# Loading two interleaved streams from two DMA queues instead of one

## The chip, the cores and the metric

The kernel runs on one core of a Trainium2 chip. The metric is the time of one execution on the device in microseconds (us). Most executions of one kernel agree within about 0.3%, so a few us of 2036 can only be judged from several runs, and stage times are read from one profiled run each. Before and the later run e4, whose traces show the same order of instructions and loads up to the end of pass 2, differed by 1.2 us at the end of pass 1 and by 2.8 us at the end of pass 2; a difference of stage times under some 3 us is not counted as shown.

Engine names are those of the profile: PE is the matmul engine (PEld its weight loads), DVE and ACT do elementwise work, POOL is GpSimd, SP is SyncE. DMA requests are made by an engine's instruction stream. A request waits there, in order, until its destination buffer is free. "Landing" is the moment when the load's last part has been reported.

## The reference

The kernel computes the output and all gradients of two rounds of attention and a squared-ReLU MLP, for one token. Nearly all bytes are the two caches, 67 MB each.

```python
def _A_ref(x, k_cache, v_cache, wq, wo):           # 32 query heads, 4 KV heads, 65536 keys, head size 128
    q = (x @ wq).reshape(B, Sq, Hq, Dh).transpose(0, 2, 1, 3)
    scores = jnp.einsum("bhqd,bhkd->bhqk", q, repeat(k_cache)) * (Dh ** -0.5)
    o = jnp.einsum("bhqk,bhkd->bhqd", _softmax(scores), repeat(v_cache))
    return o.transpose(0, 2, 1, 3).reshape(B, Sq, Hq * Dh) @ wo

def _fwd_reference(...):
    x = x + _A_ref(_layernorm(x), A_k_cache, A_v_cache, A_wq, A_wo)
    x = x + _B_ref(_layernorm(x), B_w1, B_b1, B_w2, B_b2)      # 1024 -> 3584 -> 1024
    x = x + _A_ref(_layernorm(x), A_k_cache, A_v_cache, A_wq, A_wo)
    x = x + _B_ref(_layernorm(x), B_w1, B_b1, B_w2, B_b2)
# result: x, and the vjp of this function for grad_out (gradients of both caches are 67 MB each, too)
```

## The kernel before

It makes four passes over the caches: two forward ones, a backward one that only loads (pass 3), and a backward one that loads and stores both cache gradients (pass 4). Between the passes there are dense stages for the MLP. Every big load is 1 MB and goes into one of 12 slots of the same size; 7 blocks are kept from one pass to the next. All loads are requested by SyncE.

```python
    def kv8(t, g, c8):                              # eight chunks of the K or V block that holds chunk c8
        b, j = divmod(c8, J)                        # J = 32 chunks of 128 rows in a block of 1 MB
        key = (t, g, b)
        if key not in KV["have"]:
            sl = Slot("blk_" + t)
            v = sl.t[:, :].rearrange("p (j d) -> p j d", d=DH)
            nc.sync.dma_start(out=v, in_=KVIN[t][g][b])
            KV["have"][key] = (sl, v)
        return KV["have"][key][1][:, j:j + 8, :]

    def slabs(name, load, nk, kper, ncols, ahead=1):            # wq, wo, w1, w2 in 1 MB slabs
        ...
            sl = Slot(name)
            v = sl.t[:, 0:kn * ncols].rearrange("p (k n) -> p k n", n=ncols)
            nc.sync.dma_start(out=v, in_=load(k, kn))
        ...
```

In the forward passes each step transposes eight chunks of K (kT), multiplies the ones before by the queries (kS), and multiplies much older ones by V (v8). FWD_LAG is 23 steps, so the V block of a chunk is needed 23 steps of eight chunks after its K block. A background generator (bg) slips in the matmuls of the projections with wq and wo of the other head groups, whose slabs come by the same queue.

```python
        def kT(g, c8):
            ...
            kb8 = kv8("k", g, c8)
            for i in range(8):
                nc.tensor.transpose(pt[:, i, :], kb8[:, i, :], ident_b[:, :])      # L774
            ...
        def v8(g, c8):
            vb8 = kv8("v", g, c8)
            ...
                nc.tensor.matmul(ps_o[:, 0:w, :], lhsT=vb8[:, i, :], ...)            # L858
        ...
        KV["keep"] = plan_keep(p)
        pipeline(items, [(kT, 0), (kS, TLEAD), (v8, FWD_LAG)], bg, end)
```

Pass 3 does the same with V first and K later. Each engine works through its stream in order; a scheduler of the language decides the order of the instructions on each engine at build time, from its own idea of when data arrive.

## Time and profile before

| | before |
|---|---|
| time, median of 3 | 2037.67 us (2037.56 to 2038.18) |
| passes 1, 2 and 3 (profiled run): first transpose to last product | 12.5 to 378.1, 433.3 to 781.2, 833.3 to 1197.7 us |
| DMA rate in these passes, whole slices | 406 to 416 GB/s |
| PE busy | 83% of the span |

The first view is the page of the kernel before: the mean busy share of the DMA engines and what they moved in 40 slices of 51 us each; then the two queues (q1 takes SyncE's requests, q0 GpSimd's) with packets, MB and share; then the issues with their number, KB and the median us from issue to landing.

```profile
...
DMA  9999999999999998999999986999999999999995
GB/s 384 416 410 414 413 414 415 360 335 406 411 414 413 413 415 323 398 415 410 416 412 414 416 338 231 375 424 393 422 424 424 423 423 404 423 415 423 423 371 212
...
q1 hardware_dynamic: 112190, 633.39, 76.9%
q0 software_dynamic: 24048, 165.70, 19.6%
...
blk_k<-in_A_k_cache_dram SPq DMA_DIRECT2D x248, 1024.0 KB, 20.1
blk_v<-in_A_v_cache_dram SPq DMA_DIRECT2D x243, 1024.0 KB, 20.2
...
s_wq<-in_A_wq_dram SPq DMA_DIRECT2D x32, 1024.0 KB, 18.8
s_wo<-in_A_wo_dram SPq DMA_DIRECT2D x32, 1024.0 KB, 20.2
...
```

The reader is to see two things. In passes 1 to 3 (slices 1 to 6, 9 to 14 and 17 to 22, counted from 0) the DMA is full and moves 406 to 416 GB/s. And these loads land some 20 us after their request: one queue serves loads in the order in which they were requested, with eight in flight at 2.5 us each.

The next view is what SyncE's stream waited for between 20 and 375 us of the kernel before, that is in pass 1 (us in total, times, longest).

```profile
...
SPq L282 <- DMA blk_k<-in_A_k_cache_dram: 92.4, 48, 3.2
SPq L282 <- DMA blk_v<-in_A_v_cache_dram: 73.6, 43, 2.3
SPq L282 <- PE ps_tr L774: 47.8, 36, 5.4
...
```

SyncE waits mostly for its own earlier loads, because eight are in flight, and for PE to free slots. The third view is what PE waited for between 20 and 800 us, passes 1 and 2 and the dense stages at them; only the waits for a DMA are shown.

```profile
...
PE ps_mv L397 <- DMA s_w<-in_B_w_dram: 9.0, 6, 2.4
...
PE ps_acc L858 <- DMA blk_v<-in_A_v_cache_dram: 3.8, 5, 1.5
...
PE ps_tr L774 <- DMA blk_k<-in_A_k_cache_dram: 3.3, 3, 1.4
...
```

The last view is PE's timeline at the end of pass 1 (start, us, engine, line, what, and in brackets the idle time ahead of it with its releaser).

```profile
...
358.56 0.61 PE L774 MATMUL ps_tr<-ident_b,blk_k 128*128 128x128 bf16 x8
...
374.90 1.89 PE L858 MATMUL ps_acc<-E,blk_v 128*128 128x64 bf16 x32
377.05 1.06 PE L858 MATMUL ps_acc<-E,blk_v 128*128 128x64 bf16 x32 [0.26 <-DMA blk_v<-in_A_v_cache_dram]
...
```

The last V block landed at 377.0 us, PE stood ready for it, and the pass was over 1.1 us later. The end of pass 2:

```profile
...
776.96 1.89 PE L858 MATMUL ps_acc<-E,blk_v 128*128 128x64 bf16 x32 [1.50 <-DMA blk_v<-in_A_v_cache_dram]
779.45 1.72 PE L858 MATMUL ps_acc<-E,blk_v 128*128 128x64 bf16 x32 [0.60 <-DMA blk_v<-in_A_v_cache_dram]
...
```

### The profile page before, as it was taken

Reading aid. Unit: us, or ns where it says so; the run is one execution under the profiler, and the core shown is the slowest. Engines: PE = TensorE matmul, PEld = TensorE weight load, DVE = VectorE, ACT = ScalarE, POOL = GpSimd, SP = SyncE. Lnnn points to the kernel's source line nnn. Section 1 sums busy time; section 2 is a strip of 40 time slices with the busy share of each in tenths; the row PEclk is TensorE's granted clock in tenths of the full one; section 3 lists DMA queues with packets and bytes.
Section 4 is the critical chain, followed back from the end, with each engine's and each line's share of the span. In section 5 each row is a group of like instructions: output and inputs, shape, how many; then the busy total and the mean of one; then the engine's idle time right before and its main releaser. Section 6 shows DMA issues by size and latency. Waiting matters only on the chain.

```text
span 2035.9 us, 69009 instructions
## 1 busy us (share of the span) xinstructions
PE 1689.3 (83%) x30754; PEld 1344.3 (66%) x30754; DVE 1188.6 (58%) x2586; ACT 1103.0 (54%) x2063; POOL 92.4 (5%) x232
## 2 busy tenths in 40 slices
PE   7888887688788886887978888979988978898897
PEld 6778777688787776776867777545544545454454
DVE  4444454255444542555464446867967877687775
ACT  3544454255444542445354345767766766576675
POOL 0000000000000000000000000101101111010111
PEclk9999899799899996999999988988988998698898
DMA  9999999999999998999999986999999999999995
GB/s 384 416 410 414 413 414 415 360 335 406 411 414 413 413 415 323 398 415 410 416 412 414 416 338 231 375 424 393 422 424 424 423 423 404 423 415 423 423 371 212
DMA packets 136536, 803.50 MB, mean 395 GB/s; under 512 B 12448, under 2 KB 12462, under 8 KB 52398
## 3 DMA queue, kind: packets, MB, share of 16 engines
q1 hardware_dynamic: 112190, 633.39, 76.9%
q0 software_dynamic: 24048, 165.70, 19.6%
q8 instruction: 240, 3.93, 0.8%
q14 instruction: 58, 0.48, 0.1%
HBM read 633.35 MB, written 165.69 MB: 392 GB/s over the span
## 4 chain that ended last, share of the span: by engine, by line
PE 45%; DMA 28%; ACT 15%; DVE 8%; issue 4%; SPq 0%; ACTq 0%; POOLq 0%; DVEq 0%; POOL 0%
DMA blk_v<-in_A_v_cache_dram 13%; PE ps_tr L774 7%; ACT E L831 6%; DMA blk_k<-in_A_k_cache_dram 5%; PE ps_sc L792 5%; PE ps_tr L1026 4%; PE ps_gg L1074 4%; PE ps_acc L858 4%; ACT kt L150 4%; PE ps_tr L917 3%; DVE kt L153 3%; DMA out_dram<-og 3%; PE ps_gg L1139 2%; DMA out_dram<-gstk 2%; PE ps_mv L397 2%
## 5 line engine op out<-in xcount | busy, mean ns | idle before, releaser
L153 DVE COPY kt<-ps_tr 128x1024 bf16<-128x1024 bf16 x751 | 507.3, 687 | 340.6 <-PE ps_tr L774 145.4
L150 ACT COPY kt<-ps_tr 128x1024 bf16<-128x1024 bf16 x273 | 275.7, 1024 | 410.9 <-PE ps_tr L774 230.0
L774 PE MATMUL ps_tr<-ident_b,blk_k 128*128 128x128 bf16 x4096 | 297.3, 226 | 4.3 <-DMA blk_k<-in_A_k_cache_dram 3.3
L150 ACT CAST gstk<-ps_gg 128x512 bf16<-128x512 f32 x396 | 207.6, 600 | 99.7 <-PE ps_gg L1074 78.5
L150 ACT CAST gstv<-ps_gg 128x512 bf16<-128x512 f32 x379 | 199.2, 601 | 100.1 <-PE ps_gg L1074 99.2
L774 PEld LDWEIGHTS <-blk_k 128*128 128x128 bf16 x4096 | 249.5, 102 | 4.9 <-DMA blk_k<-in_A_k_cache_dram 3.8
L792 PE MATMUL ps_sc<-L_qpad,kt 128*128 128x64 bf16 (+7 forms) x4096 | 197.4, 194 | 52.8 <-DVE kt L153 38.8
L1074 PE MATMUL ps_gg<-GG,xt 64*128 64x512 bf16 x1024 | 211.5, 403 | 21.2 <-ACT gstk L150 11.0
L792 PEld LDWEIGHTS <-kt 128*128 128x128 bf16 x4096 | 158.8, 100 | 71.3 <-DVE kt L153 45.7
L858 PE MATMUL ps_acc<-E,blk_v 128*128 128x64 bf16 (+4 forms) x4096 | 177.6, 200 | 33.0 <-issue 10.9
L1026 PEld LDWEIGHTS <-blk_v 128*128 128x128 bf16 x2048 | 128.5, 103 | 108.0 <-issue 83.0
L1026 PE MATMUL ps_tr<-ident_b,blk_v 128*128 128x128 bf16 x2048 | 183.0, 230 | 20.1 <-DMA blk_v<-in_A_v_cache_dram 18.9
L858 PEld LDWEIGHTS <-blk_v 128*128 128x128 bf16 x4096 | 152.9, 103 | 36.4 <-issue 31.3
L831 ACT ACTIVATE E<-S_sb,L_negm 128x128 bf16<-128x128 f32 x256 | 150.4, 990 | 38.2 <-DVE L_negm L827 38.1
L1101 PEld LDWEIGHTS <-blk_k 128*128 128x128 bf16 x2048 | 84.3, 100 | 115.7 <-issue 87.0
L917 PE MATMUL ps_tr<-ident_b,blk_v 128*128 128x128 bf16 x2048 | 143.7, 224 | 14.3 <-DMA blk_v<-in_A_v_cache_dram 12.0
L917 PEld LDWEIGHTS <-blk_v 128*128 128x128 bf16 x2048 | 121.4, 100 | 31.1 <-DMA blk_v<-in_A_v_cache_dram 20.6
L1101 PE MATMUL ps_acc<-X,blk_k 128*128 128x64 bf16 (+3 forms) x2048 | 119.2, 196 | 23.0 <-DMA blk_k<-in_A_k_cache_dram 23.0
L831 ACT ACTIVATION_READ_ACCUMULATOR E<-S_sb,L_negm 128x1 f32 x256 | 123.5, 483 | 0.0
L937 PE MATMUL ps_sc<-dOpad,kt 128*128 128x64 bf16 (+7 forms) x2048 | 100.7, 194 | 26.6 <-ACT kt L150 15.5
L1055 PE MATMUL ps_sc<-DOB,kt 128*128 128x64 bf16 (+3 forms) x2048 | 111.3, 198 | 0.2 <-DVE kt L153 0.2
L153 DVE CAST gstv<-ps_gg 128x512 bf16<-128x512 f32 x133 | 90.0, 684 | 28.1 <-PE ps_gg L1074 27.7
(271 smaller groups left out, 2203.0 us busy)
## 6 DMA issues: line engine op xcount, KB each, us to landing
blk_k<-in_A_k_cache_dram SPq DMA_DIRECT2D x248, 1024.0 KB, 20.1
blk_v<-in_A_v_cache_dram SPq DMA_DIRECT2D x243, 1024.0 KB, 20.2
out_dram<-gstv POOLq DMA_DIRECT2D x64, 1024.0 KB, 13.1
out_dram<-gstk POOLq DMA_DIRECT2D x64, 1024.0 KB, 12.5
s_wq<-in_A_wq_dram SPq DMA_DIRECT2D x32, 1024.0 KB, 18.8
s_wo<-in_A_wo_dram SPq DMA_DIRECT2D x32, 1024.0 KB, 20.2
s_w<-in_B_w_dram SPq DMA_DIRECT2D x32, 896.0 KB, 7.8
out_dram<-og POOLq DMA_DIRECT2D x23, 1024.0 KB, 13.9
```

The costliest lines, as they stand in the source:

```text
L150: nc.scalar.copy(out=out, in_=in_)
L153: nc.vector.tensor_copy(out=out, in_=in_)
L774: nc.tensor.transpose(pt[:, i, :], kb8[:, i, :], ident_b[:, :])
L792: nc.tensor.matmul(state["ps_s"][:, s:s + w, :].rearrange("p a b -> p (a b)"), lhsT=kt[:, i, :], rhs=L["qpad"][:, g, 0:w, :].rearrange("p ...
L831: nc.scalar.activation(out=E(g, c0, SU)[:, :, L["lr"].start + h], in_=S[:, h, :], func=ACTF.Exp, bias=negm[:, g, su, h:h + 1], scale=SCALE ...
L858: nc.tensor.matmul(ps_o[:, 0:w, :], lhsT=vb8[:, i, :], rhs=E(g, c, w)[:, :, lr], start=(c % SU == 0), stop=(c % SU == SU - 1), skip_group_ ...
L917: nc.tensor.transpose(pt[:, i, :], vb8[:, i, :], ident_b[:, :])
L937: nc.tensor.matmul(state["ps_dp"][:, s:s + w, :].rearrange("p a b -> p (a b)"), lhsT=vt[:, i, :], rhs=dOpad[:, g, 0:w, :].rearrange("p a b ...
L1026: nc.tensor.transpose(pt[:, i, :], vb8[:, i, :], ident_b[:, :])
L1055: nc.tensor.matmul(state["ps_dp"][:, s:s + w, :].rearrange("p a b -> p (a b)"), lhsT=vt[:, i, :], rhs=DOB[:, g, 0:w, :].rearrange("p a b - ...
L1074: nc.tensor.matmul(pgs[h][:, :], lhsT=xt[64 * h:64 * h + 64, j1 // 8 + m, :], rhs=gg[64 * h:64 * h + 64, :, :].rearrange("p a b -> p (a b) ...
L1101: nc.tensor.matmul(ps_dq[:, 0:w, :].rearrange("p a b -> p (a b)"), lhsT=kb8[:, i, :], rhs=X[:, s:s + w, :].rearrange("p a b -> p (a b)"), ...
```

## The change

The intent: while SyncE's stream waits for a slot or a completion, V loads can go out by a queue of their own. In passes 1 to 3 K blocks and slabs stay on SyncE, V blocks are requested by GpSimd. In pass 4 GpSimd's queue has the stores, so there all loads stay on SyncE.

```diff
-    KV = {"have": {}, "keep": set()}
+    KV = {"have": {}, "keep": set(), "two": True}
 # in kv8
-            nc.sync.dma_start(out=v, in_=KVIN[t][g][b])
+            (nc.gpsimd if t == "v" and KV["two"] else nc.sync).dma_start(out=v, in_=KVIN[t][g][b])
 # in each of the three functions that run a pass
         KV["keep"] = plan_keep(p)
+        KV["two"] = p < 3
```

The build also reorders the other engines' instructions.

More of the change, by code (lines that the diff above doesn't have):

```diff
@@ L967, in attn_bwd3 @@
         KV["keep"] = plan_keep(p)
+        KV["two"] = p < 3
         pipeline(items, [(vT, 0), (vS, TLEAD), (k8, B3_LAG)], bg, end)
@@ L1112, in attn_bwd4 @@
         KV["keep"] = plan_keep(p)
+        KV["two"] = p < 3
         pipeline(items, [(vT, 0), (vS, TLEAD), (dV8, DV_LAG), (k8, B4_LAG)], bg, end)
```

## The prediction

> **What bounds the kernel now.** The windows view gives passes 1 to 3 (about 30-360, 445-765, 840-1180 us) a DMA share of 1.01-1.02 and 408-417 GB/s; pass 4 (1280-2000 us), where GpSimd's queue stores while SyncE's loads, has slices at 423-424. SyncE's issues follow each other every 2.5 us (1 MB at 413 GB/s) and land 20 us later: eight in flight, as many as that queue has completion semaphores, so SyncE waits mostly for its own earlier DMA (215 + 207 us), else for PE to free one of 12 slots (118 + 106 us; waits view). An issue takes 0.33 us on SyncE, 0.53 us on GpSimd. Yet compute is nearly level with the DMA: PE is 80% busy and waits for blocks under 10 us in pass 1, hardly in pass 2, about 30 us in pass 3. Between passes DMA falls to 0.7-0.9 for 70-80 us, because 7 of 12 slots hold kept blocks.
>
> **What changes.** 183 V loads move from SyncE to GpSimd; no byte is saved. The Trainium skill, page "DMA: Bandwidth & Descriptors", section "Issuing engines are not separate DMA queues", says both use the same 16 engines and only issue time is saved; issue time is not the limit here. So no large gain, but four small effects:
>
> 1. Packet time. An 8 KB packet has a median of 313 ns in passes 1-3 (one queue), 309 ns in pass 4 (two): 1.3%. If two queues cause that, not the mixing of stores and loads, it is worth up to 13 us of 1000; since compute is level in passes 1 and 2, I count 5 us.
> 2. Ends of passes 1 and 2. SyncE stands 9.3 + 1.4 us at the last two V loads (slots not free), three w1 slabs queue behind, and the last V block, issued at 362.4, lands 14.6 us later. The chain of waits goes through that landing (362-377, 765-779). Now the slabs go out during the wait, and the last V blocks get their own queue's turns: same page, section "Queues, rings and completion order": each engine round-robins between queues. Landing should take 7-10 us: 11 us saved in all. The end of pass 3 waits for K blocks: nothing.
> 3. More loads in flight, limited by slots: the DMA is saturated: 0.
> 4. The scheduler reorders: PE runs V products 23.5 instead of 21.9 chunks behind the K transposes; at the start K transposes stand before the layer norm, and grad_out's load behind the first K: 2 us lost. V loads stand in GpSimd's queue behind memsets and a small store that wait for DVE; those waits ended at 427, 827 and 871 us, and the V loads after them went out at 449, 837 and 876: no loss.
>
> **Predicted time:** 2023 us, range 1995 to 2046. Faster by over 2%: 0.10; within 2%: 0.85; slower by over 2%: 0.05.
>
> **What would show it.** SyncE's waits for its own DMA nearly vanish, replaced by waits for PE. Passes 1-3 at 415-421 GB/s (413: step 1 wrong). The last V block of passes 1 and 2 lands within 10 us. Pass 4 keeps its length within 5 us.
>
> **What would make it wrong.** GpSimd's descriptors may read more slowly or be held up by DVE's copies. Sharing turns makes each block land later, holding slots longer. In-order GpSimd may stall V loads early in pass 3. If compute hides the gain, the time stays at 2037; if lag and queue depth smooth PE's stalls, it falls below 2000.

## More of the kernel before

PE waits 16 us in 780 for loads, and none of it for slabs of wq and wo.

## The result

| | before | after |
|---|---|---|
| median of 4 runs | 2037.62 us (2033.14 to 2038.18) | 2043.58 us (2042.43 to 2044.12) |
| ratio | 1 | 1.0034, 95% interval 1.002 to 1.0049 |

Ratios are the mean time of one kernel's runs over that of the other's runs of the same rounds, so they are not quite the ratio of the medians. The change costs 0.3%, where a gain of 0.7% was predicted.

Where the time went, from the two profiled runs (end of each stage in us; the last column is what the stage itself added):

| end of | before | after | after - before | added |
|---|---|---|---|---|
| start (first K transpose) | 12.5 | 14.8 | +2.2 | +2.2 |
| pass 1 (last V product) | 378.1 | 386.0 | +7.9 | +5.7 |
| dense stage | 433.3 | 440.1 | +6.9 | -1.0 |
| pass 2 | 781.2 | 795.5 | +14.4 | +7.5 |
| dense stage | 833.3 | 847.9 | +14.6 | +0.2 |
| pass 3 | 1197.7 | 1212.1 | +14.5 | -0.1 |
| dense stage | 1255.7 | 1265.4 | +9.7 | -4.8 |
| pass 4 | 2013.1 | 2020.5 | +7.4 | -2.3 |
| end | 2035.9 | 2042.4 | +6.4 | -1.0 |

So passes 1 and 2 lost 13 us, the start 2 us, and the dense stage ahead of pass 4 gave 5 us back. The page of the kernel after, same lines as before:

```profile
...
DMA  9999999799999998999999997999999999999995
GB/s 384 416 400 415 408 415 416 303 353 398 410 415 400 416 409 314 370 413 411 416 411 416 397 380 270 361 423 393 422 424 423 423 423 406 424 424 424 419 380 212
...
q1 hardware_dynamic: 85982, 442.54, 53.9%
q0 software_dynamic: 50256, 356.55, 42.3%
...
blk_k<-in_A_k_cache_dram SPq DMA_DIRECT2D x248, 1024.0 KB, 23.0
blk_v<-in_A_v_cache_dram POOLq DMA_DIRECT2D x182, 1024.0 KB, 12.0
...
s_wq<-in_A_wq_dram SPq DMA_DIRECT2D x32, 1024.0 KB, 22.9
s_wo<-in_A_wo_dram SPq DMA_DIRECT2D x32, 1024.0 KB, 21.3
...
```

The rate in the passes is nearly what it was (397 to 416 GB/s in the same slices). What changed are the landings: V blocks now come 12.0 us after the request instead of 20.2, K blocks 23.0 us instead of 20.1, slabs of wq 22.9 us instead of 18.8. (These medians are of the whole run, pass 4 included for K and for V before; between 60 and 340 us, in pass 1, V took 13.2 us and K 22.3, against 20.2 and 20.1 before.) In 19 of the 33 stretches of 10 us between 30 and 360 us each queue moved 199 to 215 GB/s, 410 to 417 together. The other stretches are uneven, most of them where one queue had little to do; but from 350 to 360 us V's queue moved 297 GB/s and SyncE's 110 with two or more loads in flight on each, so equal shares are what was mostly seen here, not a rule. SyncE's waits in pass 1:

```profile
...
SPq L282 <- PE ps_tr L774: 167.1, 40, 11.3
SPq L351 <- PE ps_acc L858: 63.9, 9, 16.1
...
SPq L282 <- DMA s_wq<-in_A_wq_dram: 6.8, 2, 5.9
...
```

The waits for its own loads are nearly gone, as predicted (9.6 us are left, all for slabs); it waits for slots now. PE's waits for DMA in passes 1 and 2:

```profile
...
PE ps_bg L397 <- DMA s_wq<-in_A_wq_dram: 40.3, 6, 12.0
...
PE ps_bg L397 <- DMA s_wo<-in_A_wo_dram: 13.7, 5, 3.7
PE ps_tr L774 <- DMA blk_k<-in_A_k_cache_dram: 12.3, 7, 4.0
...
PE ps_mv L397 <- DMA s_w<-in_B_w_dram: 5.5, 4, 2.1
...
```

PE now waits 54 us for slabs of wq and wo, for which it never waited before. And PE's timeline at the end of pass 1:

```profile
...
375.06 0.38 PE L825 MATMUL ps_mv<-ident_f,gmb 8*128 8x8 f32 x2 [0.62 <-DVE gmb L823]
380.40 5.57 PE L858 MATMUL ps_acc<-E,blk_v 128*128 128x64 bf16 x128 [4.96 <-ACT L_fw L879]
...
```

The last V block landed at 375.0 us, 2.0 us earlier than before, but PE had 128 V products left and had waited for ACT just before; the pass ended at 386.0 us. The end of the pass is 11 us behind the bytes.

One more measure will decide the matter: the **lead** of a load, from its landing to PE's first use of it. It was worked out from the traces by pairing the landings of a pass's K blocks (or V blocks) in order with the uses of the blocks in order. Median leads in pass 1: K 3.8 us before and 3.8 us after; V 4.4 us before and 14.4 us after, and never under 7.7 us.

### The profile page after: what moved, and what is told of

Same layout as the page of the kernel before. It is cut to its first block, busy times and chain, and to the rows that moved or that the text cites. A ratio compares the mean times of both kernels' runs of the same rounds, so it can differ in the third digit from the quotient of the medians. Undisturbed runs are those within 1.5% of the kernel's fastest.

```text
span 2042.4 us, 69103 instructions
## 1 busy us (share of the span) xinstructions
PE 1664.2 (81%) x30754; PEld 1337.5 (65%) x30754; DVE 1181.2 (58%) x2586; ACT 1101.3 (54%) x2064; POOL 188.5 (9%) x414
## 4 chain that ended last, share of the span: by engine, by line
PE 40%; DMA 40%; ACT 10%; DVE 6%; issue 3%; SPq 0%; POOLq 0%; ACTq 0%; DVEq 0%
DMA blk_k<-in_A_k_cache_dram 15%; DMA blk_v<-in_A_v_cache_dram 10%; PE ps_tr L774 7%; DMA s_wq<-in_A_wq_dram 5%; ACT E L831 5%; PE ps_acc L858 5%; PE ps_tr L1028 4%; DMA s_wo<-in_A_wo_dram 4%; PE ps_sc L792 4%; PE ps_gg L1076 3%; PE ps_tr L918 3%; DVE kt L153 2%; PE ps_gg L1142 2%; DMA out_dram<-og 2%; DMA out_dram<-gstk 2%
## 5 line engine op out<-in xcount | busy, mean ns | idle before, releaser
L153 DVE COPY kt<-ps_tr 128x1024 bf16<-128x1024 bf16 x751 | 516.4, 688 | 428.5 <-PE ps_tr L774 233.7
L774 PE MATMUL ps_tr<-ident_b,blk_k 128*128 128x128 bf16 x4096 | 340.8, 227 | 29.4 <-DMA blk_k<-in_A_k_cache_dram 21.2
L774 PEld LDWEIGHTS <-blk_k 128*128 128x128 bf16 x4096 | 255.4, 102 | 34.0 <-DMA blk_k<-in_A_k_cache_dram 22.5
L858 PE MATMUL ps_acc<-E,blk_v 128*128 128x64 bf16 (+4 forms) x4096 | 203.3, 198 | 62.2 <-ACT al L840 36.5
L1076 PE MATMUL ps_gg<-GG,xt 64*128 64x512 bf16 x1024 | 213.3, 410 | 14.8 <-ACT gstk L150 4.4
L792 PE MATMUL ps_sc<-L_qpad,kt 128*128 128x64 bf16 (+7 forms) x4096 | 215.2, 195 | 5.8 <-issue 5.7
L858 PEld LDWEIGHTS <-blk_v 128*128 128x128 bf16 x4096 | 162.9, 102 | 66.1 <-issue 65.9
L1028 PEld LDWEIGHTS <-blk_v 128*128 128x128 bf16 x2048 | 128.6, 103 | 111.0 <-issue 83.4
L1028 PE MATMUL ps_tr<-ident_b,blk_v 128*128 128x128 bf16 x2048 | 184.0, 231 | 20.8 <-DMA blk_v<-in_A_v_cache_dram 19.8
L792 PEld LDWEIGHTS <-kt 128*128 128x128 bf16 x4096 | 178.6, 101 | 8.8 <-issue 6.9
L282 POOL DMA_DIRECT2D blk_v<-in_A_v_cache_dram x182 | 96.2, 529 | 928.3 <-PE ps_acc L858 377.7
L918 PE MATMUL ps_tr<-ident_b,blk_v 128*128 128x128 bf16 x2048 | 167.7, 227 | 7.9 <-issue 7.9
L1103 PEld LDWEIGHTS <-blk_k 128*128 128x128 bf16 x2048 | 85.2, 101 | 115.6 <-issue 89.8
L958 PE MATMUL ps_acc<-dsT,blk_k 128*128 128x64 bf16 (+7 forms) x2048 | 107.4, 196 | 61.1 <-DMA blk_k<-in_A_k_cache_dram 53.2
L918 PEld LDWEIGHTS <-blk_v 128*128 128x128 bf16 x2048 | 127.0, 102 | 8.7 <-issue 8.4
L958 PEld LDWEIGHTS <-blk_k 128*128 128x128 bf16 x2048 | 82.3, 101 | 65.8 <-DMA blk_k<-in_A_k_cache_dram 59.8
## 6 DMA issues: line engine op xcount, KB each, us to landing
out_dram<-gstv POOLq DMA_DIRECT2D x64, 1024.0 KB, 13.4
s_wq<-in_A_wq_dram SPq DMA_DIRECT2D x32, 1024.0 KB, 22.9
```

Source lines behind the costliest of these rows:

```text
L153: nc.vector.tensor_copy(out=out, in_=in_)
L282: (nc.gpsimd if t == "v" and KV["two"] else nc.sync).dma_start(out=v, in_=KVIN[t][g][b])
L792: nc.tensor.matmul(state["ps_s"][:, s:s + w, :].rearrange("p a b -> p (a b)"), lhsT=kt[:, i, :], rhs=L["qpad"][:, g, 0:w, :].rearrange("p ...
L858: nc.tensor.matmul(ps_o[:, 0:w, :], lhsT=vb8[:, i, :], rhs=E(g, c, w)[:, :, lr], start=(c % SU == 0), stop=(c % SU == SU - 1), skip_group_ ...
L918: nc.tensor.transpose(pt[:, i, :], vb8[:, i, :], ident_b[:, :])
L958: nc.tensor.matmul(ps_dq[:, 0:w, :].rearrange("p a b -> p (a b)"), lhsT=kb8[:, i, :], rhs=dsT[:, s:s + w, :].rearrange("p a b -> p (a b)") ...
```

## The experiments

All kernels gave correct results. Times are medians, each ratio is against runs of the kernel before on the same chip. Most of the experiments are **pinned**: each instruction of PE, ACT and DVE is put behind the one that stands ahead of it in a given order, by edges that only order and never wait, so that nothing but the queues differs:

```python
    for text in ORDERS:                                     # orders of PE, ACT, DVE, packed
        for i in instructions_in_that_order(text):
            if last is not None:
                tc.add_manual_dep(i, last.name, mybir.DependencyInfo(mybir.DependencyClass.NoSync, ...))
            last = i
```

The traces confirm the orders: PE's 30754 instructions stand in the order of before in e1, e5 to e7, e9 to e11 and e13 to e18, and in the order of after in e2.

The theories in the order in which they came: A, the scheduler's new order costs the time. B, its rival in the first four runs: the transfers themselves do, since slabs and K land later. C, V is served ahead of K at the ends of the passes. E, compute runs level with the DMA and can't make up a late start or a stall. D, the rival throughout: the path through GpSimd costs by itself. G, the last: two queues that share the rate equally deliver in another order than the one in which data are needed.

### 1 to 3: the scheduler's order

Run e1 has the queues of after and the instruction order of before; e2 the queues of before and the order of after; e3 is after with the first matmul of each background slab kept in program order, because the traces showed these standing about ten chunks earlier in PE's stream than before.

```diff
 e1: after + pinned to the order of before        e2: before + pinned to the order of after
 e3: in g_mv
-                nc.tensor.matmul(ps[:, :, nb], ...)
+                mm = nc.tensor.matmul(ps[:, :, nb], ...)
+                if nb == 0 and ps_of is ps_bg:
+                    tc.keep_in_program_order(mm)
```

> The changed kernel's queues (V blocks of passes 1 to 3 on GpSimd's), but PE, ACT and DVE held to the order that they have in the kernel before. Theory A (the 6 us are lost because the scheduler, given two queues, puts the first wq slab's products of a head group some 10 chunks earlier in PE's order, ahead of K blocks that land sooner, so PE stands 11-12 us four times): the time falls to 2025-2038 us, the four long waits of PE for wq slabs are gone. Theory B (the loss is of the transfers themselves: with each queue at 206 GB/s, SyncE's slabs and K blocks land later, 22-25 instead of 20 us): the time stays at 2042-2050 us.

> The reverse: all blocks on SyncE's queue as in the kernel before, but PE, ACT and DVE held to the order of the changed kernel. Theory A: slower than the kernel before, 2043-2060 us, with PE waiting over 8 us for the first wq slab of groups 3 and 4 in passes 1 and 2. Theory B: the order is harmless, 2033-2040 us.

> The changed kernel, with the first of each eight background products of a weight slab pinned behind what stands before it on PE in program order; in the build the first wq slab's products of groups 3 and 4 go from K chunk 74 to 81-84 and from 137 to 145-148. Theory A: the four long waits shrink to a few us and most of the loss of passes 1 and 2 comes back, 2028-2038 us. Theory B: 2042-2048 us.

Measured: e1 2047.57 us, 1.0052 (1.0038 to 1.0066); e2 2037.79 us, 1.0008 (0.9995 to 1.0021); e3 2042.29 us, 1.0026 (1.0012 to 1.0039). The order alone costs nothing that can be measured, the queues alone cost 0.5%, and all three times lie in B's ranges. Theory A falls; B is not yet a mechanism, and C and G are its heirs. PE's waits for wq between 20 and 800 us in e2 (one queue, new order):

```profile
...
PE ps_bg L397 <- DMA s_wq<-in_A_wq_dram: 36.0, 4, 12.5
...
```

These are 36 us of the very waits that looked so bad in after, and e2 lost 2.5 us by the end of pass 2 and nothing that shows in the time. A wait of PE in this kernel is not yet a loss: what lands meanwhile is used up faster afterwards. In e1 PE's waits for wo are these:

```profile
...
PE ps_bg L397 <- DMA s_wo<-in_A_wo_dram: 12.7, 3, 6.3
...
PE ps_tr L774 <- DMA blk_k<-in_A_k_cache_dram: 1.6, 2, 0.8
...
```

They are fewer, 12.7 us, and yet pass 1 ended 8.2 and pass 2 13.2 us late. The waits do not size the loss.

One rival was not on the list: the granted clock of PE. In passes 1 and 2 (30 to 360 and 445 to 765 us) it was 0.94 and 0.95 before and only 0.90 and 0.91 in after. The runs settle it: e1 was granted 0.93 and 0.95, nearly as before, and lost as much; e2 was granted 0.91 and 0.94 and lost nothing that shows.

### 4: only in pass 3

```diff
-        KV["two"] = p < 3
+        KV["two"] = p == 2
```

> V blocks on GpSimd's queue in pass 3 alone. Passes 1 and 2 should be as in the kernel before. Both theories: pass 3 itself no faster (364 us in both traces), and if the 5 us that the changed kernel gained between the end of pass 3 and the start of pass 4 belong to pass 3's queues, the time is 2030-2034 us; if they belong to something else, 2036-2039.

Measured: 2035.86 us, 0.9995 (0.9978 to 1.0012). With V on GpSimd in pass 3 alone (and all loads on SyncE until then) nothing is lost; the loss belongs to passes 1 and 2.

### 5 to 8: which loads go to GpSimd's queue

Run e5 leaves the last 12 V blocks of passes 1 and 2 on SyncE; e6 sends pairs of loads to the two queues in turn; e7 sends K to GpSimd in passes 1 and 2 (the first needed stream, as V is in pass 3); e8 is e7 with the order left free. e5 to e7 are pinned to the order of before.

```diff
 e5: -  nc.gpsimd if t == "v" and KV["two"]
     +  nc.gpsimd if t == "v" and KV["two"] and not late          # late: place 52 or more of the pass's 64
 e6: +  nc.gpsimd if KV["n"] // 2 % 2 and KV["two"]                # n counts the loads
 e7: +  nc.gpsimd if t == ("v" if KV["pass"] == 2 else "k") and KV["two"]
```

> As the run with two queues and the old order (2047.6 us), but the last 12 V blocks of passes 1 and 2 go back to SyncE's queue. Theory C (the DMA moves as many bytes per us as before, but V, which is needed 22 chunks later than K, gets half the engines and lands after 10-12 us while K takes 22-25; V is then two or three blocks ahead, the last K block of a pass lands 7 us later, and the work that must follow it stands bare): V's lead is gone by the end of the pass, the last K block of pass 1 lands at 356-359 us instead of 364, and the time falls to 2033-2041 us. Theory D (GpSimd's path itself costs: its issues, its in-order waits, its descriptors): most blocks still take it, so 2044-2048 us.

> Old order of PE, ACT and DVE; in passes 1 to 3 the loads go to the two queues by turns, two by two, so that each queue carries K and V alike and half of all blocks still come through GpSimd. Theory C: blocks land nearly in the order of need; K and V take about the same time to land (15-22 us), and the time is 2034-2041 us. Theory D: as many blocks through GpSimd as in the changed kernel, so 2043-2049 us.

> Old order of PE, ACT and DVE; in passes 1 and 2 K (needed first) goes to GpSimd's queue and V stays on SyncE's with the weight slabs; pass 3 as in the changed kernel (V first, on GpSimd). Theory C: K lands early (10-13 us), V late (22-25 us); the last K block of pass 1 lands before 357 us, V's landing ends pass 1 at 377-381 us as in the kernel before, time 2030-2041 us. Theory D: 2044-2049 us, since the same number of blocks goes through GpSimd.

> The same queues, but with the order that the scheduler makes of it. Order alone moved the time by 0.08% (the one-queue run with the new order), so Theory C: 2030-2042 us; it may beat the kernel before by a few us if the dense stage after pass 3 gains the 3-5 us seen in the changed kernel. Theory D: 2043-2050 us.

Measured: e5 2050.29 us, 1.0054 (1.0034 to 1.0074); e6 2052.01 us, 1.0073 (1.0054 to 1.0092); e7 2059.31 us, 1.0113 (1.0096 to 1.0131); e8 2060.8 us, 1.0117 (1.0098 to 1.0137). In e5 the last K block landed at 355.6 us and the last V block at 377.4 us, within 1 us of before (356.5, 377.0), and still pass 1 ended at 385.8 us. PE's timeline of e5 shows why: its last K transposes ended at 367.0 us, 7.9 us later than before, although their block had landed at 355.6, and the work after them took as long as before (18.8 us, 18.9 before). The last V products are of blocks that had landed; they waited for the softmax (ACT), not for a load:

```profile
...
366.42 0.61 PE L775 MATMUL ps_tr<-ident_b,blk_k 128*128 128x128 bf16 x8
...
376.81 1.87 PE L859 MATMUL ps_acc<-E,blk_v 128*128 128x64 bf16 x32 [3.69 <-ACT L_fw L880]
...
382.97 2.87 PE L859 MATMUL ps_acc<-E,blk_v 128*128 128x64 bf16 x64
...
```

Theory C falls: the last landings are not the cause. Every way of sharing the loads out lost, and all four runs were slower than the ranges of both theories. But e6 to e8 can't say what their sharing costs: the 2 KB load of grad_out came late in them, PE stood 17.4, 25.0 and 18.9 us for it at the start, and in e6 and e7 the first K transpose came 12.3 and 20.0 us late.

### 9 to 12: a late start, and the slabs

In the two-queue runs the start is later: SyncE's stream has the first K load ahead of the 2 KB load of grad_out, whose transpose stands ahead of the layer norm on PE. Run e9 is e1 with the start of before (grad_out's load first, the first two V loads on SyncE); e10 adds the slabs of wq and wo to GpSimd's queue; e12 is e10 with free order; e11 is the kernel before with nothing but grad_out's load put behind five K loads.

```diff
 e9:  +  tc.add_manual_dep(load.ins, KV["gx"].name, <order only>)             # a K load after grad_out's
      +  (nc.gpsimd if t == "v" and KV["two"] and not first else nc.sync)      # first: the first two V loads
 e10: +  (nc.gpsimd if KV["slab"] and KV["m"] > 4 and name in ("s_wq", "s_wo") else nc.sync).dma_start(out=v, in_=load(k, kn))
 e11: +  if KV["n"] == 5:                                                       # one queue
      +      tc.add_manual_dep(KV["gx"], load.ins.name, <order only>)         # grad_out's after the fifth K load
```

> Both pinned to the old instruction order; against the first run (two queues, old order: ratio 1.0052) only the start is undone: the load of grad_out goes ahead of every K load again, and the first two V blocks stay on SyncE's queue, so that the first 25 us are as before. Theory E (compute runs level with the DMA and never catches up, so what the start loses stays): the first K transpose is back at 12.5 us instead of 17.1, pass 1 ends about 3 to 4 us later than before instead of 8.2, and the time is near 2042 us, ratio about 1.003. Rival D (the path through GpSimd costs by itself): unchanged, pass 1 ends 8 us late, ratio about 1.005.

> As the run before it, and the 1 MB slabs of wq and wo of passes 1 to 3 (after the first four) go to GpSimd's queue too, which has the smaller backlog. Theory E: slabs land after 10 to 15 us instead of 20 to 28, PE no longer waits 5 to 6 us for them in passes 1 and 2, pass 1 ends within 2 us of before and pass 2 loses under 2 us; ratio 0.998 to 1.002. Rival D: more loads on GpSimd, so slower than the run before it, ratio 1.005 or more.

> One queue and the old instruction order, that is the kernel before, with one edit: the 2 KB load of grad_out is put behind the first five K loads. No GpSimd load at all in passes 1 to 3. Theory E: the first K transpose comes about 12 us later (near 24 us), and pass 1 ends 10 to 12 us later although the queue loads as fast; the time grows by 8 to 12 us, ratio 1.004 to 1.006. Rival D, and the view that the passes are simply bound by bytes: the queue keeps loading while PE waits, PE catches up, pass 1 ends within 2 us of before, ratio within 1.001.

> The same queues as the second run of this set, with the instruction order left to the scheduler: a candidate for a better version. Theory E: like the second run, 0.997 to 1.002; with the earlier placing of the slabs' matmuls costing nothing where slabs land in time. Rival D: 1.004 or more.

Measured: e9 2050.37 us, 1.0075 (1.0052 to 1.0098); e10 2062.51 us, 1.0134 (1.0115 to 1.0153); e11 2040.1 us, 1.0018 (1.0 to 1.0036); e12 2070.08 us, 1.0164 (1.0143 to 1.0184). In e9 the first K transpose was back at 12.5 us (17.1 in e1), and pass 1 ended 8.7 us late all the same. In e11 the first transpose came 12.4 us late, yet pass 1 ended only 3.8 us late. PE's waits in e11:

```profile
...
PE ps_mv L161 <- DMA rows_c<-in_grad_out_dram: 17.7, 1, 17.7
...
PE ps_tr L777 <- DMA blk_k<-in_A_k_cache_dram: 3.1, 6, 0.8
...
```

The first line is the delay that was made on purpose. Neither theory's range was hit, but E is much further off. Afterwards PE made up 8.6 of 12.4 us, because the queue had filled the slots meanwhile, in the right order; what stayed, 3.8 us, is what the loads themselves lost when all slots were full (the first 60 MB were there 3.4 us late, the first 140 MB 3.5 us). Theory E falls: compute can catch up, if the data are the right ones. That left D against a new theory, G: in pass 1 the pinned two-queue runs e1, e9 and e10 had received each number of bytes up to 140 MB within 0.6 us of the time of before, so what PE lacked was not bytes, but the right ones.

### 13 and 14: the order without GpSimd, and GpSimd without the order

Run e13 has one queue, SyncE's. The only edit is the order of its requests: every V load stands where it had landed in e1, which is in the median 2 loads earlier than before. That takes over the start of e1 too: a K load stands ahead of grad_out's, and the first K transpose came at 17.3 us. Run e14 has one queue too, GpSimd's: K, V and all slabs up to pass 4, in the order that SyncE's queue had before. Both are pinned to the old order on PE, ACT and DVE.

```diff
 e13: before + the order of SyncE's requests pinned to the order of landing of e1
 e14: -  (nc.gpsimd if t == "v" and KV["two"] else nc.sync).dma_start(out=v, in_=KVIN[t][g][b])
      +  (nc.gpsimd if KV["two"] else nc.sync).dma_start(out=v, in_=KVIN[t][g][b])
      -  nc.sync.dma_start(out=v, in_=load(k, kn))
      +  (nc.gpsimd if KV["two"] else nc.sync).dma_start(out=v, in_=load(k, kn))
      +  the order of GpSimd's requests pinned to the order of SyncE's before
```

> All loads on SyncE's queue, none of passes 1 to 3 on GpSimd, instruction order of the other engines as before; only the order of the requests on SyncE is changed: each V load stands where it landed in the run with two queues and the old order, which is about 2 loads earlier than before. Theory G (two queues share the rate equally, so V lands ahead of need and K and the slabs behind it; compute falls back by the lead that V gains and the end of each byte-bound pass shows it): the loss comes back without GpSimd. Median time from V's landing to its first use in pass 1 rises from 4.4 us to 12 or more, pass 1 ends 6 to 9 us later, pass 2 10 to 14 us later, ratio 1.003 to 1.006. Rival D (the path through GpSimd costs by itself): no loss, within 2 us at the end of both passes, ratio within 1.001.

> One queue again, but GpSimd's: K, V and every weight slab up to the start of pass 4 are requested by GpSimd in the old order of SyncE's queue. Theory G: the old order of landing is back, so passes 1 and 2 end within 3 us of before (start and issue aside), V's median time from landing to use is near 4 us again, ratio 0.999 to 1.002. Rival D: 473 loads through GpSimd instead of 182, so a larger loss than with V alone, 1.006 or more.

Measured: e13 2044.42 us, 1.0041 (1.0023 to 1.0058), V's median lead in pass 1 16.8 us, passes 1 and 2 ended 4.5 and 8.5 us late. Its waits of PE for DMA between 20 and 800 us:

```profile
...
PE ps_bg L397 <- DMA s_wo<-in_A_wo_dram: 14.8, 3, 7.4
...
PE ps_tr L774 <- DMA blk_k<-in_A_k_cache_dram: 0.4, 1, 0.4
...
```

The waits for wo are those of e1, without one load of GpSimd in these passes. In the whole time the loss is nearly that of e1 (1.0052); by the ends of passes 1 and 2 it is 4.5 of 8.2 and 8.5 of 13.2 us, less than I had expected. In pass 1 the order can't be told from the start: PE was 4.8 us late at the first K block and 4.9 at the last, while in e11 it had made up most of a later start. Pass 2 has no such start, and there e13 added 4.0 us, e1 5.0. In both, PE's lateness steps up at one wait for a slab of wo: of 6.3 us at 643 us in e1, of 6.4 at 639 in e13. e14: 2052.48 us, 1.0086 (1.0071 to 1.0101), but passes 1 and 2 ended 0.9 and 0.6 us late, with V's median lead at 2.5 us. Its waits of PE:

```profile
...
PE ps_tr L774 <- DMA blk_k<-in_A_k_cache_dram: 6.4, 8, 1.4
...
PE ps_acc L858 <- DMA blk_v<-in_A_v_cache_dram: 4.6, 5, 2.6
...
```

No wait for wq or wo, although all of them came by GpSimd. The median 8 KB packet took 313 ns in pass 1 on either queue. By the ratio alone D's range (1.006 or more) was hit and G's missed; the stages speak for G, since the loss of e14 is all after pass 2: from 340 to 350 MB, ahead of pass 3, the loads fell 12 us behind, where GpSimd's stream stood 18 us at a small store that waited for DVE, and slab requests stood ahead of the blocks.

### 15 and 17 and 18: two queues, with the lead of V held back

These are e1 again, two queues and the old order, with one thing added: a V request on GpSimd waits until a load that stood ahead of it in the old order has landed: the second one ahead (e15), the third (e17), or the fourth (e18). The order of SyncE's requests is that of before without V, which also gives back the early start (first K transpose at 12.4 us in all three).

```diff
+    for v, w in GATES:                       # V load, and the 2nd, 3rd or 4th load ahead of it
+        tc.add_manual_dep(by_name["I-%d" % v], "I-%d" % w, mybir.DependencyInfo(mybir.DependencyClass.Sync, ...))
```

> Two queues as in the first run of the study (old instruction order, ratio 1.0052), but each V request on GpSimd waits until the second load ahead of it in the old order has landed, so V can't run ahead. Theory G: V's median time from landing to use falls from 17.8 us to 4 to 9 us in pass 1, passes 1 and 2 end 1 to 5 us later than before instead of 8 and 13, ratio 1.000 to 1.003. Rival D: the same loads by the same path and one more wait each, so no better than 1.005.

> As the gated run, but each V request waits for the third load ahead of it in the old order instead of the second, since there V came too late (13 us of waits for V at PE in passes 1 and 2, median 2.3 us from landing to use). Theory G: V's median lead in pass 1 is 4 to 10 us, waits of PE for V vanish without those for slabs coming back, passes 1 and 2 end 0 to 5 us late, ratio 1.000 to 1.003. If the ratio stays at 1.005, two queues lose also with V's lead as before, and theory G doesn't explain all.

> As the last gated run (third load ahead: ratio 0.9987, V's median lead 3.8 us in pass 1), but each V request waits for the fourth load ahead of it, so V may run one load further ahead. Theory G: V's median lead in pass 1 rises to 7 to 12 us, passes 1 and 2 end 2 to 6 us later than with the third, and the ratio is between those of the third and of no gate, 1.000 to 1.004. If the gate itself, and not V's lead, is what helps, the ratio stays at 0.998 to 0.999.

Measured: e15 2044.7 us, 1.0047 (1.0033 to 1.0061); e17 2032.3 us, 0.9987 (0.9974 to 1.0001); e18 2036.68 us, 1.001 (0.9995 to 1.0025). PE's waits for DMA (other than w1 and w2) between 20 and 800 us. In e15, which missed G's ranges, V now comes too late:

```profile
...
PE ps_acc L858 <- DMA blk_v<-in_A_v_cache_dram: 13.3, 9, 3.6
...
```

In e17 both sides are small (V's lead of 3.8 us is just under G's range, the ratio better than it):

```profile
...
PE ps_acc L858 <- DMA blk_v<-in_A_v_cache_dram: 7.6, 3, 4.3
...
PE ps_bg L397 <- DMA s_wo<-in_A_wo_dram: 0.7, 1, 0.7
PE ps_bg L397 <- DMA s_wq<-in_A_wq_dram: 0.5, 1, 0.5
...
```

In e18 the slabs come late again:

```profile
...
PE ps_bg L397 <- DMA s_wo<-in_A_wo_dram: 13.2, 4, 4.4
...
PE ps_bg L397 <- DMA s_wq<-in_A_wq_dram: 3.0, 1, 3.0
...
```

Here are all the runs that bear on it. Leads are medians in us; "late" is the end of the pass against before; "waits" are PE's for V blocks and for wq and wo between 20 and 800 us.

| run | queues | V's lead, pass 1 / 2 | pass 1 late | pass 2 late | waits for V | for wq, wo | ratio |
|---|---|---|---|---|---|---|---|
| before | SyncE | 4.4 / 8.1 | 0 | 0 | 3.8 | 0 | 1 |
| e2, new order | SyncE | 5.3 / 6.1 | 1.2 | 2.5 | 3.5 | 38.9 | 1.0008 |
| e14, all on GpSimd | GpSimd | 2.5 / 6.6 | 0.9 | 0.6 | 4.6 | 0 | 1.0086 (pass 3) |
| e17, gate 3 | both | 3.8 / 5.1 | 3.5 | 0.8 | 7.6 | 1.2 | 0.9987 |
| e15, gate 2 | both | 2.3 / 5.8 | 5.4 | 13.3 | 13.3 | 0 | 1.0047 |
| e18, gate 4 | both | 9.1 / 11.1 | 5.0 | 4.8 | 0 | 16.2 | 1.0010 |
| e13, landing order of e1 | SyncE | 16.8 / 16.7 | 4.5 | 8.5 | 0 | 14.8 | 1.0041 |
| after | both | 14.4 / 14.0 | 7.9 | 14.4 | 0 | 54.0 | 1.0034 |
| e1, old order | both | 17.8 / 15.4 | 8.2 | 13.2 | 0 | 13.2 | 1.0052 |

The two queues are there in e17 as in e1, and so is GpSimd's path with all its loads. What differs is when V may be requested, and the loss is gone (the start differs too, but e9 has it as e17 does and lost 0.75%). The 3.5 us in pass 1 come at one block for which even this gate was too tight: PE was 0.9 us late until it stood 4.3 us for V at 317 us, and 3.4 us late after it. Over pass 2 e17 lost nothing, where e1 added 5.0 us. With the next looser gate V's lead in pass 1 rises from 3.8 to 9.1 us, the waits for slabs are back, and passes 1 and 2 end 5.0 and 4.8 us late instead of 3.5 and 0.8; only the second difference is larger than that between two like runs. The ratio lies between (its interval still touches that of e17). With a gate that is too tight it is V that is late. So it is not the gate as such that helps, but the order.

### 16: one queue on GpSimd in passes 1 and 2 only

This is e14 with SyncE's queue again from the end of pass 2, to keep GpSimd's stream out of the start of pass 3.

```diff
+        KV["two"] = p < 1            # at the end of each forward pass
```

> As the run with everything on GpSimd's queue, but only until the end of pass 2 (296 loads, K, V and slabs); from there on all loads are on SyncE's queue again as before. In the run up to pass 4, passes 1 and 2 ended 0.9 and 0.6 us late and 12 us were lost at the start of pass 3, where GpSimd's stream holds a store and slab requests that wait. Theory G: the whole is as before, ratio 0.999 to 1.002. Rival D: 296 loads through GpSimd where the change makes 120 in these passes, so 1.005 or more.

Measured: 2039.61 us, 1.003 (1.0013 to 1.0047), with a wide spread (2038.12 to 2047.23). Theory G's range for the ratio was missed. Pass 1 ended 1.2 us late, pass 2 7.0 us. PE's waits for V between 20 and 800 us:

```profile
...
PE ps_acc L858 <- DMA blk_v<-in_A_v_cache_dram: 9.1, 4, 6.8
...
```

The longest, 6.8 us, is at the last V block of pass 2: it was requested at 760.5 us and landed at 786.4; in e14 at 760.0 and 780.0. In e16 two w1 slabs had been requested on SyncE's queue at 765.7 and 769.1 us, and at once took turns with GpSimd's backlog of seven loads, one of them about to land. It is the same effect at another place, made by my edit; it was read from the trace and not tested by itself.

## Why the prediction was wrong

**Step 1, packet time (5 us counted): wrong.** The median 8 KB packet of pass 1 took 313 ns with two queues, on both of them, as with one; the passes ran at 406 to 412 GB/s, 410 to 414 before. The 309 ns of pass 4 are there with and without the change and don't come from a second queue as such; the mixing of loads and stores is what is left, not tested.

**Step 2, the ends of passes 1 and 2 (11 us counted): this is the step that failed.** The prediction took the last V block's landing for what ends the pass, and expected a landing within 10 us of the request. It took 14.5 us (360.5 to 375.0; 16.0 in pass 2), was still 2.0 us earlier than before, and the pass ended 7.9 us later. The chain through that landing was real before, but a second path was as long: PE had stood for the last V blocks only 0.26 us in pass 1 and 2.1 us in pass 2, so by these waits an earlier landing could bring an estimated 2 to 3 us, not 11. What sets the end is when PE gets through its last K transposes, since in pass 1 some 19 us of work follow them in the runs with the old order: 18.9 before, 19.2 in e1, 18.8 in e5, 18.6 in e17. They ended at 359.2 us before, at 367.1 in e1 and at 363.0 in e17. "Each engine round-robins between queues" was mostly right (199 to 215 GB/s each in 19 of 33 stretches). Its consequence was taken for the last block only, where it seemed to help, and not for the 360 us before it.

**What the runs showed in its place.** V is needed 23 steps after K, so in the old order a V load stands behind many K loads. With a queue of its own it got about half of the rate in most stretches with work on both, and landed 12 to 13 us after its request while K and the slabs, with the long queue, took 21 to 23 us. The rate is nearly the same, so what V is early the others are late. Shown: this order, on SyncE's queue alone, brings back most of the loss of the whole time (1.0041 of 1.0052) and of pass 2 (4.0 of 5.0 us), while in pass 1 the start blurs it (e13); GpSimd's path with the old order costs under 1 us in passes 1 and 2 (e14); and two queues with V's lead held to that of before lose nothing (e17, with e15 and e18 on both sides of it). The size is argued only: V's lead grew by 10.0 us in after; at 206 GB/s that is an estimated 2.1 MB which lie in slots too early, 5 us at 413 GB/s, of 5.7 us that pass 1 itself lost. In e1 the same estimate gives 13.4 us, 2.8 MB, 6.7 us, of 8.2 late. For e17 it gives nothing and 3.5 us were measured at the end of pass 1, for e13 6.2 and 4.5 us, start included, so it is good to some 4 us. A pass's end shows it and the dense stage can't pay it back; pass 2 starts anew and loses again.

**Step 3, more loads in flight (0): right.** SyncE's waits for its own K and V loads vanished (166 us in pass 1 before) and were worth nothing.

**Step 4, the scheduler's order (2 us lost) and GpSimd's stream (no loss): right in size.** The start lost 2.2 us, the order alone 0.08% with an interval around zero (e2), and GpSimd's stream did not stall V. But the match at the start is luck as far as the whole time goes, for e9 and e11 show that a late start is not a term of the sum: undone, it brought nothing back, and 12.4 us of it cost 3.8.

**What would make it wrong:** "Sharing turns makes each block land later, holding slots longer" came closest. Blocks of K did land later, and V's slots held data that waited 14.4 us for their use; the harm came by the order of landing, which the sentence does not name.

The sum was -5 - 11 + 2; measured in the stages are +2.2 at the start, +13.2 in passes 1 and 2, and -9.0 later, of which -4.8 is the dense stage ahead of pass 4. That gain was not predicted. It came in e1 too (-5.4), but e4, which has the change in pass 3 alone, shows no gain in its time (0.9995), and in e16, which has one queue there, the stage was 4.8 us shorter too. Its cause is open. Open too is the rest of the loss that e13 did not bring back (3.7 us in pass 1, 4.7 us in pass 2), and what made e10 and e12 so slow; there V waits of 11.7 us (e10) point at V standing behind slabs in GpSimd's stream, which was not tested.

A version better than both: e17 beats after clearly and is 0.13% below before, but its interval reaches 1.0001; it may be taken as equal to before, and the one queue is simpler.

## What to carry to other kernels

When a kernel is bound by DMA bytes, as these passes are, the order in which a queue delivers is a resource: here one queue kept the order of need, and two queues favoured the one with the shorter backlog, whatever was needed first. Before streams are split, look at each stream's lead from landing to first use; here it was 4 us on one queue, and the split stopped costing time only with a gate on the stream that is needed later (a request waits for the landing of the third load ahead of it). And before a landing is counted as the end of a stage, look at how long the engine stood for it: 0.26 us here, where 14.6 us of the chain went through the landing. And a new wait on the compute engine is no measure of a loss: 36 us of waits cost nothing in e2, while 13 us went with 13 us lost in e1, where V filled the slots early.

## What the Trainium skill lacked or had wrong

- Page "DMA: Bandwidth & Descriptors", section "Issuing engines are not separate DMA queues": it says that loads of all issuing engines run on the same 16 DMA engines and that issuing from several only saves issue time. This case agrees on the rate (199 to 215 GB/s on each queue in 19 of 33 stretches of pass 1, 410 to 417 together, 406 to 416 with one) but not on the "only": the split changed the order of landing (in pass 1 V from 20.2 to 13.2 us after the request, K from 20.1 to 22.3) and cost 0.3 to 0.5%.
- The same page, section "Queues, rings and completion order": it states that each DMA engine round-robins between queues at packet granularity. The equal shares in most stretches agree (350 to 360 us, 297 against 110 GB/s, does not show them). What it lacks is the consequence seen here: a load in the queue with the shorter backlog overtakes earlier requests in the other. In e16 two slabs on SyncE's queue, requested at 765.7 and 769.1 us, landed at 775.0 and 778.9, ahead of the last two V blocks on GpSimd's, which had been requested at 756.1 and 760.5 us, and the last V block landed 26.0 us after its request, 20.0 in e14.
- The same page, section "SWDGE vs HWDGE vs iDMA": it warns that GpSimd's descriptors may be held up by DVE, and calls the hardware path faster to set up. No cost of this kind was seen with 1 MB loads: with every load of passes 1 and 2 on GpSimd these passes ended within 1 us of before, at 313 ns per 8 KB packet on either path. (The page ties the hold-up to a mode of DVE; whether DVE was in it was not looked at.) An issue took 0.53 us on GpSimd and 0.33 us on SyncE.
- No page that I read has the measure, the lead from a load's landing to its first use for each stream: 4.4 us for V before, 14.4 us after.
